# Two feed-forward layers after clustered attention: three chunks of 512 tokens in place of four of 384

## The chip, the cores and the metric

The kernel runs on one core of a Trainium2 chip. The metric is the device time of one execution in microseconds (us). Matrix products run on TensorE (PE; the loads of its stationary operand are listed apart as PEld). VectorE is DVE, ScalarE is ACT, GpSimd is POOL, and SP issues most transfers.

## The reference, cut to what matters

```python
x = attention(q, k, v, centroids)      # 2 x 8 heads x 768 tokens x 64, keys masked by cluster
x = x.reshape(1536, 512)               # tokens x model width
x = (relu(x @ w_in) ** 2) @ w_out      # layer 0: 512 -> 2048 -> 512
h = x @ w_in2
out = (h * sigmoid(1.702 * h)) @ w_out2   # layer 1: 512 -> 2048 -> 512
```

All inputs are float32.

## The kernel before

Each engine executes its instructions in the order in which they are recorded. That order comes from a list of events: `at(key, f)` files a piece of work under a number, the list is sorted by that number, and the pieces are then emitted. Keys are not times; they only decide who stands ahead of whom. Attention has keys up to about 99; for the layers, `moment(u)` turns a position u, counted in units, into a key.

A float32 product is made of three products of rounded parts: every operand is split into a high half (the value rounded to the type float32r) and a low half (value minus high half), and the sum is high x high + low x high + high x low. So each block of a product costs three matmuls.

Tokens are held with the model width on the partitions, in four chunks of 384 (`xhl`, one per half of a batch). The hidden width of 2048 is cut into 16 blocks of 128 (`m`). Each layer has two stretches:

- **Hidden stretch.** For each block m and chunk c one unit: `hidden` issues 12 matmuls (3 products x 4 slices of the model width) into one of eight PSUM banks. `inner` and `outer` apply the activation and store the value in `g_t[m][:, c]`. In layer 0 both run on ACT; in layer 1 ACT makes the sigmoid and DVE multiplies it with the bank.
- **Output stretch.** It is done twice, each time for 768 tokens (g = 0, 1). For each m and half s, `g_high` (ACT) and `g_low` (DVE) split the stored value into the two halves, in a ring of three buffers (`ghl`), and `reduce_out` adds the matmuls of block m into banks that stay open over all 16 blocks. In layer 0 the token chunk is the moving operand (384 columns, line 696); in layer 1 it is the weight tile (512 columns, line 702). Then `leave_high` and `leave_low` write the next layer's x, or `leave` copies a tile of the result, which a transfer takes to memory.

A weight tile (512 x 128 values) comes from memory as 64-bit words. `w_stages` lists its preparation: a transfer of 512 KB by SP into one of two places; `magnitude` on ACT (line 193); `clamp`, `shift`, `join_low`, `join_high` on DVE (lines 196, 200, 204, 208); `high` on ACT (line 212); `low` on POOL (line 215), which subtracts the high half from the value. There are 32 tiles per layer. `weights` files these eight pieces one after another from a position `first` on. Ten places of 4 KB are for tiles; in the output stretch six more tiles lie where chunks 2 and 3 of x lay, and two in places of the w_in tiles.

The first units of layer 0 use batch 0 only and stand among the last pieces of attention: `values` of the last half (24 matmuls into `ps_v`), `ratio`, `whole`, `whole_high`, `whole_low`, whose keys are in the table `LAST`.

Of the kernel before, what the change touches and what calls it, by code (L numbers as in the profile page):

```python
# [8 lines left out]
F32 = mybir.dt.float32  # L9
# [7 lines left out]
P = 128  # L17
# [24 lines left out]
    values=(97.86, 97.96, 98.06, 98.16, 98.26, 98.36), inverse=(95.9, 95.9), spread=(96.2, 96.2), ratio=97.85, ratio_out=98.2,  # L42
    whole=98.9, whole_high=98.95, whole_low=99.2,
# [22 lines left out]
def cluster_attention_then_two_ffns(  # L66
# [30 lines left out]
    NC = B * 2  # L97
# [4 lines left out]
    assert NT == 6 and D == 64 and KD * P == DM and MF == 16 and NC == 4  # L102
# [5 lines left out]
    ROOM = {F32R: 97 * KB, F32: 110 * KB + 512}  # L108
# [51 lines left out]
    g_at = [14 * KB + 512 + 6 * KB * m for m in range(MF)]  # L160
    g_t = [view(a, [NC, HALF]) for a in g_at]
    r_p, tmp, o_p = Places(0, 4608), Places(4608, 4608 + 6 * KB), Places(0, g_at[0])
    words_at = 10 * KB + 512
# [3 lines left out]
    def slot_of(layer, which, m):  # L167

        ring = slots[8:] if layer == 0 else slots[:2]
        rest = slots[:8] if layer == 0 else slots[2:]  # L170
        if which == 0:
            return rest[7] if layer == 0 and m == 2 else ring[m % 2]
        return rest[m] if m < 8 else x_slots[m - 8] if m < 14 else ring[m - 14]

    def weight(layer, which, m):
        return view(slot_of(layer, which, m), [2, DM], F32R)
# [44 lines left out]
    with tc.manual_schedule():  # L221
        with ExitStack() as actx:
# [9 lines left out]
            oht_p = view(12 * KB * 2 + 3 * KB, [S], F32R, 4 * C)  # L232
            oh_p = view(12 * KB * 3 + 3 * KB, [NT, 4, C], F32R)
            ident_r = view(12 * KB * 3 + 4 * KB + 512, [P], F32R)
            oh0_p = view(12 * KB * 2 + 9 * KB, [NT, 4, 2 * C], F32R)
# [350 lines left out]
            def whole(n):  # L586
                p, u = divmod(n, 2)
                b, hp = PAIRS[p]
                x = rb_t[n]
                nc.vector.tensor_tensor(out=x, in0=pv_t.pop(n)[:, :HALF], in1=x, op=ALU.mult)  # L590

            def whole_high(n):
                p, u = divmod(n, 2)
                b, hp = PAIRS[p]
                nc.scalar.copy(out=xhl[2 * b + u][:, 0, hp, :], in_=rb_t[n])

            def whole_low(n):
                p, u = divmod(n, 2)
                b, hp = PAIRS[p]
                x, t = rb_t.pop(n), xhl[2 * b + u]  # L600
                nc.vector.tensor_tensor(out=t[:, 1, hp, :], in0=x, in1=t[:, 0, hp, :].bitcast(F32), op=ALU.subtract)
# [28 lines left out]

            H_LEN, Y_LEN = MF * NC, 2 * MF
            LAYER = H_LEN + 2 * Y_LEN
# [5 lines left out]
            def open_banks():  # L638
                actx.close()
                pool = ctx.enter_context(tc.tile_pool(name="psum2", bufs=1, space=bass.MemoryType.PSUM, reuse_waits="tile"))  # L640
                banks.extend(pool.tile([P, 512], F32, name=f"bank{i}") for i in range(8))

            def bank(i):
                return banks[i % 8]

            def hidden(layer, u, m, c):
                if banks:
                    ps = bank(u)
# [5 lines left out]
                w, x = weight(layer, 0, m), xhl[c]  # L654
# [7 lines left out]
            r_t = {}  # L662

            def inner(layer, m, c):
                r = r_t[layer, m, c] = r_p.tile([P, HALF], F32, tag="r", bufs=3)
                ps = ps_u[layer, m, c][:, :HALF]
                if layer == 0:
                    nc.scalar.activation(out=r, in_=ps, func=AF.Relu)
                else:
                    nc.scalar.activation(out=r, in_=ps, func=AF.Sigmoid, scale=1.702)  # L670

            def outer(layer, m, c):
                r, ps = r_t.pop((layer, m, c)), ps_u.pop((layer, m, c))
                if layer == 0:
                    nc.scalar.activation(out=g_t[m][:, c, :], in_=r, func=AF.Square)
                else:
                    nc.vector.tensor_tensor(out=g_t[m][:, c, :], in0=ps[:, :HALF], in1=r, op=ALU.mult)  # L677


            def half_of(g, m, s):  # L680
                return ghl[((g * MF + m) * 2 + s) % 3]

            def g_high(g, m, s):
                nc.scalar.copy(out=half_of(g, m, s)[:, 0, :], in_=g_t[m][:, 2 * g + s, :])  # L684

            def g_low(g, m, s):
                t = half_of(g, m, s)
                nc.vector.tensor_tensor(out=t[:, 1, :], in0=g_t[m][:, 2 * g + s, :], in1=t[:, 0, :].bitcast(F32), op=ALU.subtract)  # L688

            def reduce_out(layer, g, m, i):  # L690
                w = weight(layer, 1, m)
                if layer == 0:
                    s, d = divmod(i, KD)
                    t = half_of(g, m, s)
                    for e, (a, b) in enumerate(((0, 0), (1, 0), (0, 1))):
                        nc.tensor.matmul(bank(i)[:, :HALF], lhsT=w[:, a, d * P:(d + 1) * P], rhs=t[:, b, :],  # L696
                                         start=(m == 0 and e == 0), stop=(m == MF - 1 and e == 2))
                else:
                    s, i_ = divmod(i, TH)
                    t = half_of(g, m, s)  # L700
                    for e, (b, a) in enumerate(((0, 0), (0, 1), (1, 0))):
                        nc.tensor.matmul(bank(NT * g + i), lhsT=t[:, b, i_ * P:(i_ + 1) * P], rhs=w[:, a, :],  # L702
                                         start=(m == 0 and e == 0), stop=(m == MF - 1 and e == 2))

            def leave_high(g, i):
                s, d = divmod(i, KD)
                nc.scalar.copy(out=xhl[2 * g + s][:, 0, d, :], in_=bank(i)[:, :HALF])

            def leave_low(g, i):
                s, d = divmod(i, KD)  # L710
                x = xhl[2 * g + s]
                nc.vector.tensor_tensor(out=x[:, 1, d, :], in0=bank(i)[:, :HALF], in1=x[:, 0, d, :].bitcast(F32), op=ALU.subtract)

            def leave(g, i):
                o = o_p.tile([P, DM], F32, tag="o", bufs=7)
                rows, ps = out[g * S + i * P:g * S + (i + 1) * P], bank(NT * g + i)
                if g == 1 and i == NT - 1:
# [7 lines left out]
            def weights(layer, which, m, first, pitch=0.3):  # L725
# [108 lines left out]
```

## Time and profile before

| | us |
|---|---|
| median of 3 runs (lowest, highest) | 798.59 (796.96, 798.88) |
| profiled execution: its own time | 797.05 |
| its span, first to last instruction | 795.3 |
| PE busy in the span | 781.6 (98%) |
| DVE, ACT, POOL busy | 460.0, 437.1, 203.4 |

The span is what the profile's rows add up to; what lies around it in the execution's own time is 1.75 us. Busy time of PE says that matmuls are in flight, not that they are at their peak.

### The profile page before, as it was taken

The page shows a single profiled execution, that of the slowest core. Times are in us where ns is not written, and L with a number is a line of the kernel's source. Part 1 is how long each engine was busy: PE and PEld are TensorE (multiplying, and loading weights), DVE is VectorE, ACT ScalarE, POOL GpSimd, SP SyncE. Part 2 cuts the span into 40 slices and gives each one's busy share as a digit, 9 for nine tenths or more (in the row PEclk, how much of TensorE's full clock was granted, in tenths as well). Part 3 has the DMA queues.
Part 4 walks back from the last instruction along what each step waited for, and adds up shares of the span by engine and source line. Part 5 has one row for each costly group of instructions (what it writes and reads, how often), then busy time and mean ns, then how long its engine had stood idle before and what let it go on. Part 6 is the DMA issues. An engine that isn't in the chain of part 4 may idle for free.

```text
span 795.3 us, 12110 instructions
## 1 busy us (share of the span) xinstructions
PE 781.6 (98%) x4523; PEld 685.8 (86%) x4523; DVE 460.0 (58%) x865; ACT 437.1 (55%) x859; POOL 203.4 (26%) x158
## 2 busy tenths in 40 slices
PE   7899999999999999999999999999999999999998
PEld 5766766766776899999999999999999998888886
DVE  6657877877877353545266555755655445663222
ACT  6777887877866476767534344453433333443222
POOL 2564754754601122222011101201211110110000
PEclk9799999999999999999999999999999999999999
DMA  4232332331220133333012201211322101212002
GB/s 140 71 92 58 87 79 56 94 82 46 58 66 28 54 106 107 98 91 130 9 72 80 80 27 55 85 48 56 105 80 78 55 28 54 79 54 80 0 1 80
DMA packets 18202, 54.61 MB, mean 69 GB/s; under 512 B 2720, under 2 KB 2976, under 8 KB 18144
## 3 DMA queue, kind: packets, MB, share of 16 engines
q1 hardware_dynamic: 17856, 53.32, 21.8%
q8 instruction: 35, 0.57, 0.3%
q10 hardware_dynamic: 288, 0.52, 0.2%
q14 instruction: 23, 0.19, 0.1%
HBM read 43.02 MB, written 3.15 MB: 58 GB/s over the span
## 4 chain that ended last, share of the span: by engine, by line
PE 93%; ACT 3%; DVE 2%; issue 1%; POOL 1%; DMA 0%; POOLq 0%; ACTq 0%; DVEq 0%
PE bank L658 31%; PE bank L696 17%; PE bank L702 16%; PE ps_v L562 8%; PE ps_p L544 7%; PE ps_s L519 4%; PE ps_s L522 4%; PE ps_h L658 2%; ACT arena L536 1%; PE ps_aff L380 1%; DVE arena L528 1%; PE ps_r L579 1%; PE ps_back L397 1%; PE ps_oh L463 1%; PE ps_aff L383 0%
## 5 line engine op out<-in xcount | busy, mean ns | idle before, releaser
L658 PE MATMUL bank<-arena 128*128 128x384 f32 x1440 | 249.9, 334 | 0.0
L658 PEld LDWEIGHTS bank<-arena 128*128 128x128 f32 x1440 | 249.6, 188 | 0.0
L215 POOL TENSOR_TENSOR arena<-arena,arena 128x512 fp32r<-128x512 f32 x64 | 82.6, 1291 | 393.8 <-ACT arena L212 349.9
L688 DVE TENSOR_TENSOR arena<-arena,arena 128x384 fp32r<-128x384 f32 x128 | 78.4, 613 | 126.4 <-ACT arena L684 125.3
L684 ACT CAST arena<-arena 128x384 fp32r<-128x384 f32 x128 | 65.8, 514 | 140.5 <-PE bank L702 76.1
L696 PE MATMUL bank<-arena 128*128 128x384 f32 x768 | 133.3, 334 | 0.0
L696 PEld LDWEIGHTS bank<-arena 128*128 128x128 f32 x768 | 133.1, 188 | 0.0
L702 PE MATMUL bank<-arena 128*128 128x512 f32 x576 | 130.8, 389 | 0.0
L702 PEld LDWEIGHTS bank<-arena 128*128 128x128 f32 x576 | 108.1, 188 | 22.4
L528 DVE TENSOR_SCALAR_CACHE_REDUCE arena<-ps_s 128x768 bf16<-128x768 f32 x96 | 91.8, 956 | 43.2 <-PE ps_s L522 37.2
L536 ACT ACTIVATE arena<-ps_s,arena 128x768 f32<-128x768 f32 x96 | 87.0, 906 | 38.2 <-DVE arena L528 37.9
L544 PE MATMUL ps_p<-arena 128*128 128x128 f32 x576 | 72.7, 277 | 0.0
L562 PE MATMUL ps_v<-arena 128*64 128x384 f32 x384 | 72.1, 498 | 0.0
L196 DVE TENSOR_SCALAR arena<-arena 128x512 f32<-128x512 f32 x64 | 34.6, 541 | 61.8 <-ACT arena L193 61.5
L544 PEld LDWEIGHTS ps_p<-arena 128*128 128x128 f32 x576 | 67.8, 144 | 2.4 <-issue 0.6
L677 DVE TENSOR_TENSOR arena<-bank,arena 128x384 f32<-128x384 f32 x64 | 35.6, 556 | 58.9 <-ACT arena L670 58.9
L670 ACT ACTIVATE arena<-bank 128x384 f32<-128x384 f32 x64 | 31.5, 492 | 69.3 <-PE bank L658 69.3
L519 PE MATMUL ps_s<-arena 128*128 128x384 f32 x192 | 55.6, 371 | 4.8 <-ACT arena L536 4.8
L212 ACT CAST arena<-arena 128x512 fp32r<-128x512 f32 x64 | 39.7, 620 | 34.0 <-DVE arena L208 33.9
L522 PE MATMUL ps_s<-arena 80*128 80x384 f32 x192 | 50.9, 346 | 0.6 <-ACT arena L474 0.5
L519 PEld LDWEIGHTS ps_s<-arena 128*128 128x128 f32 x192 | 31.7, 192 | 21.7 <-ACT arena L536 10.1
L552 DVE COPY arena<-ps_p 128x512 f32<-128x512 f32 x72 | 47.0, 677 | 1.0 <-PE ps_p L544 0.9
(95 smaller groups left out, 745.5 us busy)
## 6 DMA issues: line engine op xcount, KB each, us to landing
arena<-in_w_dram SPq DMA_DIRECT2D x64, 512.0 KB, 3.3
arena<-arena SPq DMA_DIRECT2D x32, 192.0 KB, 2.5
arena<-in_k_t_dram SPq DMA_DIRECT2D x8, 384.0 KB, 3.8
arena<-in_v_dram SPq DMA_DIRECT2D x8, 384.0 KB, 3.3
out_dram<-arena SPq DMA_DIRECT2D x11, 256.0 KB, 2.1
arena<-in_q_t_dram SPq DMA_DIRECT2D x7, 384.0 KB, 3.4
arena<-arena SPq DMA_DIRECT2D x28, 48.0 KB, 2.1
arena<-in_q_t_dram ACTq DMA_DIRECT2D x1, 384.0 KB, 3.0
```

What stands on the lines that cost most here:

```text
L215: nc.gpsimd.tensor_tensor(out=halves[:, 1, :], in0=x[0].bitcast(F32), in1=halves[:, 0, :].bitcast(F32), op=ALU.subtract)
L519: nc.tensor.matmul(ps[:, n, :HALF], lhsT=x_s[i][:, t * P:(t + 1) * P], rhs=k1_s[i][:, n * HALF:(n + 1) * HALF], start=True, stop=False)
L522: nc.tensor.matmul(ps[:, n, :HALF], lhsT=q2_s[i][:, t * P:(t + 1) * P], rhs=k2_s[i][:, n * HALF:(n + 1) * HALF], start=False, stop=True)
L528: nc.vector.tensor_scalar(out=unused, in0=s_t[g][:, :, :HALF], scalar1=-scale, scalar2=None, op0=ALU.mult, op1=ALU.min, accum_out=m_t[g])
L536: nc.scalar.activation(out=p_t[g].rearrange("p (n f) -> p n f", n=2), in_=s_t.pop(g)[:, :, :HALF], func=AF.Exp, bias=m_t.pop(g), scale=sca ...
L544: nc.tensor.transpose(ps[:, x * P:(x + 1) * P], p_t[2 * k + j][:, t * P:(t + 1) * P], ident)
L562: nc.tensor.matmul(pv_t[n][j * D:(j + 1) * D, :HALF], lhsT=raw[n // 2, "v"][:, j, t, :], rhs=pt_t[n, j][:, t, :], start=(t == 0), stop=(t ...
L658: nc.tensor.matmul(ps[:, :HALF], lhsT=w[:, a, kk * P:(kk + 1) * P], rhs=x[:, b, kk, :], start=(n == 0), stop=(n == 3 * KD - 1))
L684: nc.scalar.copy(out=half_of(g, m, s)[:, 0, :], in_=g_t[m][:, 2 * g + s, :])
L688: nc.vector.tensor_tensor(out=t[:, 1, :], in0=g_t[m][:, 2 * g + s, :], in1=t[:, 0, :].bitcast(F32), op=ALU.subtract)
L696: nc.tensor.matmul(bank(i)[:, :HALF], lhsT=w[:, a, d * P:(d + 1) * P], rhs=t[:, b, :], start=(m == 0 and e == 0), stop=(m == MF - 1 and e ...
L702: nc.tensor.matmul(bank(NT * g + i), lhsT=t[:, b, i_ * P:(i_ + 1) * P], rhs=w[:, a, :], start=(m == 0 and e == 0), stop=(m == MF - 1 and e ...
```

## The change

The tokens are held as one tensor `xf` (halves x model slices x 1536 tokens) and cut into three chunks of 512. A hidden unit still has 12 matmuls, now 512 columns wide, and there are 48 units per layer, not 64. The output stretch takes chunk 0 alone first (16 units, four banks), then chunks 1 and 2 together (32 units, eight banks), in both layers; its units have 12 matmuls of 512 columns, too. The activation is written to `g_t` in place. Eight w_out tiles (m = 8 to 15) lie where chunks 1 and 2 of x lay, and are prepared while the sums of chunk 0 are made, one every 1.6 units; before, such a tile came every 3.2 units of 12 matmuls of 384 columns. Nine other places hold tiles. Chunk 1 spans both batches, so the first six units stand in another order, and `LAST` has other keys. Every key of the layers' work is new.

```diff
 LAST = dict(
-    values=(97.86, 97.96, 98.06, 98.16, 98.26, 98.36), inverse=(95.9, 95.9), spread=(96.2, 96.2), ratio=97.85, ratio_out=98.2,
-    whole=98.9, whole_high=98.95, whole_low=99.2,
+    values=(97.1, 97.2, 97.3, 97.4, 97.5, 97.6), inverse=(95.9, 95.9), spread=(96.2, 96.2), ratio=97.05, ratio_out=97.4,
+    whole=97.95, whole_high=98.0, whole_low=98.1,
 )
...
-    xhl = [view(12 * KB * c, [2, KD, HALF], F32R) for c in range(NC)]
-    slots = [60 * KB + 4 * KB * i for i in range(7)] + [48 * KB + 4 * KB * i for i in range(3)]
-    x_slots = [24 * KB + 4 * KB * i for i in range(6)]
-    ghl = [view(88 * KB + 3 * KB * i, [2, HALF], F32R) for i in range(3)]
...
+    xf = view(0, [2, KD, B * S], F32R)
+    slots = [view(48 * KB + 4 * KB * i, [2, DM], F32R) for i in range(9)]
+    x_slots = [xf[:, :, kk, c * CH:(c + 1) * CH] for c in (1, 2) for kk in range(KD)]
+    ghl = [view(84 * KB + 4 * KB * i, [2, CH], F32R) for i in range(3)]
...
-                        nc.tensor.matmul(ps[:, :HALF], lhsT=w[:, a, kk * P:(kk + 1) * P], rhs=x[:, b, kk, :],
+                        nc.tensor.matmul(ps, lhsT=w[:, a, kk * P:(kk + 1) * P], rhs=xf[:, b, kk, c * CH:(c + 1) * CH],
...
+            def half_of(m, c):
+                return ghl[(MF + 2 * m + c - 1 if c else m) % 3]
...
+            def sums(layer, c, i):
+                return bank(layer, (0, 4, 8)[c] + i)
+
+            def reduce_out(layer, m, c, i):
+                w, t, ps = weight(layer, 1, m), half_of(m, c), sums(layer, c, i)
+                cols = slice(i * P, (i + 1) * P)
+                for e, (a, b) in enumerate(((0, 0), (1, 0), (0, 1))):
+
+                    lhsT, rhs = (w[:, a, cols], t[:, b, :]) if layer == 0 else (t[:, a, cols], w[:, b, :])
+                    nc.tensor.matmul(ps, lhsT=lhsT, rhs=rhs, start=(m == 0 and e == 0), stop=(m == MF - 1 and e == 2))
...
-            def weights(layer, which, m, first, pitch=0.3):
+            def weights(layer, which, m, first, pitch=0.25):
...
-                at(moment(first - 2.7), load_w)
+                at(moment(first - 1.9), load_w)
...
                     if m >= 8:
-                        jobs.append((y0 + 3.6 + 3.2 * (m - 8), 1, m))
+                        jobs.append((y0 + 0.3 + 1.6 * (m - 8), 1, m))
...
+                    order[:6] = [(0, 0), (1, 0), (0, 1), (1, 1), (0, 2), (1, 2)]
...
+                u = y0
+                for part in PARTS:
                     for m in range(MF):
...
+                        for c in part:
+                            at(moment(u - 1.4), g_high, m, c)
+                            at(moment(u - 1.1), g_low, m, c)
+                            for i in range(4):
+                                at(moment(u + 0.25 * i), reduce_out, layer, m, c, i)
+                            u += 1
```

What this does to the order is seen at two places. On PE, where layer 0 goes from its hidden to its output stretch, before (`bank` is a PSUM bank; x12 counts equal rows in a row):

```order
L658 MATMUL bank6_2697<-arena_99328_58 128x384 x12
L658 MATMUL bank7_2698<-arena_99328_58 128x384 x12
L696 MATMUL bank0_2691<-arena_99328_58 128x384 x3
L696 MATMUL bank1_2692<-arena_99328_58 128x384 x3
L696 MATMUL bank2_2693<-arena_99328_58 128x384 x3
L696 MATMUL bank3_2694<-arena_99328_58 128x384 x3
L696 MATMUL bank4_2695<-arena_99328_58 128x384 x3
```

and at the same place after the change:

```order
L656 MATMUL bank2_2634<-arena_98304_58 128x512 x12
L656 MATMUL bank3_2635<-arena_98304_58 128x512 x12
L695 MATMUL bank4_2636<-arena_98304_58 128x512 x3
L695 MATMUL bank5_2637<-arena_98304_58 128x512 x3
L695 MATMUL bank6_2638<-arena_98304_58 128x512 x3
L695 MATMUL bank7_2639<-arena_98304_58 128x512 x3
L695 MATMUL bank4_2636<-arena_98304_58 128x512 x3
```

Block m = 0 now has four banks and 12 matmuls before block 1 follows in the same banks; before it had eight banks and 24 narrower matmuls.

On ACT, in the first output stretch of layer 0, where w_out tiles are prepared, before (line 193 is `magnitude`, 212 the `high` half of a tile, 684 `g_high`):

```order
L193 ACTIVATE arena_59<-arena_59 128x512
L684 CAST arena_58<-arena_59 128x384
L212 CAST arena_58<-arena_59 128x512
L684 CAST arena_58<-arena_59 128x384 x2
L193 ACTIVATE arena_59<-arena_59 128x512
```

and after (191, 210 and 679 are the same three), around the tile m = 13, whose `high` is the first of the two rows of line 210:

```order
L191 ACTIVATE arena_59<-arena_59 128x512
L679 CAST arena_58<-arena_59 128x512
L210 CAST arena_58<-arena_59 128x512
L679 CAST arena_58<-arena_59 128x512
L191 ACTIVATE arena_59<-arena_59 128x512
L679 CAST arena_58<-arena_59 128x512 x2
L210 CAST arena_58<-arena_59 128x512
```

The `g_high` behind that `high` is the one of unit 11 of the 16. DVE does for the same tile, after the change (194 `clamp`, 198 `shift`, 202 and 206 the joins, 683 `g_low`):

```order
L194 TENSOR_SCALAR arena_59<-arena_59 128x512
L198 TENSOR_SCALAR arena_59<-arena_59 128x512
L683 TENSOR_TENSOR arena_58<-arena_59,arena_58 128x512
L202 SCALAR_TENSOR_TENSOR arena_59<-arena_59 128x512
L206 SCALAR_TENSOR_TENSOR arena_59<-arena_59 128x512
L683 TENSOR_TENSOR arena_58<-arena_59,arena_58 128x512
L194 TENSOR_SCALAR arena_59<-arena_59 128x512
```

Per tile there are now one or two `g_low` between one `clamp` and the next, the second of the two here being that of unit 11; before there were about three.

## Rows read from the trace of the kernel before

**Rows 1.** The page: busy time, share of the span and instructions of each engine.

```profile
PE 781.6 (98%) x4523; PEld 685.8 (86%) x4523; DVE 460.0 (58%) x865; ACT 437.1 (55%) x859; POOL 203.4 (26%) x158
```

**Rows 2.** End of the chain that ended last: start us, us, engine, tile, line, count.

```profile
256.68 4.38 PE ps_h L658 x24
261.39 4.02 PE ps_v L562 x24
265.41 12.70 PE ps_h L658 x72
278.12 116.48 PE bank L658 x672
394.60 133.12 PE bank L696 x768
527.72 133.12 PE bank L658 x768
660.83 130.62 PE bank L702 x576
```

**Rows 3.** Groups by line and shape: count, busy us, mean ns, idle us before.

```profile
L658 PE MATMUL bank<-arena 128*128 128x384 f32 x1440 | 249.9, 334 | 0.0
L702 PE MATMUL bank<-arena 128*128 128x512 f32 x576 | 130.8, 389 | 0.0
```

**Rows 4.** Busy time by stretch: us, PE, PEld, DVE, ACT, POOL (instructions), clock, DMA.

```profile
256.60:394.30 137.70, 137.70 (x797) 135.10 (x796) 60.60 (x98) 89.24 (x176) 29.72 (x23) 1.00 0.26 85
394.30:527.30 133.00, 133.00 (x769) 133.00 (x768) 78.81 (x140) 57.23 (x111) 20.62 (x16) 1.00 0.21 68
...
791.40:795.30 3.90, 0.04 (x1) 0.00 (x0) 0.42 (x1) 0.37 (x1) 0.00 (x0) 1.00 0.64 232
```

**Rows 5.** Instructions in order of time, 401 to 407 us, one w_out tile.

```profile
401.12 0.67 ACT L193 ACTIVATE arena<-arena 128x512 f32<-128x512 f32 x1
...
401.82 0.43 DVE L196 TENSOR_SCALAR arena<-arena 128x512 f32<-128x512 f32 x1
402.28 0.43 DVE L200 TENSOR_SCALAR arena<-arena 128x512 int32<-128x512 int32 x1
402.74 0.69 DVE L204 SCALAR_TENSOR_TENSOR arena<-arena 128x512 int32<-128x512 int32 x1
...
403.35 0.55 DVE L688 TENSOR_TENSOR arena<-arena,arena 128x384 fp32r<-128x384 f32 x1
403.82 0.69 DVE L208 SCALAR_TENSOR_TENSOR arena<-arena 128x512 int32<-128x512 int32 x1
404.54 0.62 ACT L212 CAST arena<-arena 128x512 fp32r<-128x512 f32 x1 [1.25 <-DVE arena L208]
...
405.07 0.51 ACT L684 CAST arena<-arena 128x384 fp32r<-128x384 f32 x1
405.24 1.29 POOL L215 TENSOR_TENSOR arena<-arena,arena 128x512 fp32r<-128x512 f32 x1 [22.19 <-ACT arena L212]
405.61 1.33 DVE L688 TENSOR_TENSOR arena<-arena,arena 128x384 fp32r<-128x384 f32 x1 [1.10 <-ACT arena L684]
```

**Rows 6.** DVE in order of time, 268 to 269 us: joins back to back.

```profile
268.17 0.69 DVE L204 SCALAR_TENSOR_TENSOR arena<-arena 128x512 int32<-128x512 int32 x1
268.90 0.69 DVE L208 SCALAR_TENSOR_TENSOR arena<-arena 128x512 int32<-128x512 int32 x1
```

**Rows 7.** Single lines: duration ns min/median/max, first and last start.

```profile
L196 DVE TENSOR_SCALAR arena<-arena x64: 427/428/1067, 235.0 to 712.9; 128x512 f32<-128x512 f32 x64
...
L688 DVE TENSOR_TENSOR arena<-arena,arena x128: 548/559/1341, 391.4 to 785.7; 128x384 fp32r<-128x384 f32 x128
...
L677 DVE TENSOR_TENSOR arena<-bank,arena x64: 545/558/558, 531.7 to 661.4; 128x384 f32<-128x384 f32 x64
```

**Rows 8.** POOL and DVE in order of time, near 280 us.

```profile
279.79 1.30 POOL L215 TENSOR_TENSOR arena<-arena,arena 128x512 fp32r<-128x512 f32 x1 [6.04 <-ACT arena L212]
...
280.30 1.07 DVE L196 TENSOR_SCALAR arena<-arena 128x512 f32<-128x512 f32 x1 [1.90 <-ACT arena L193]
```

**Rows 9.** Transfers: line, queue, count, KB each, median us to landing.

```profile
arena<-in_w_dram SPq DMA_DIRECT2D x64, 512.0 KB, 3.3
```

More of the change, by code (lines that the diff above doesn't have):

```diff
@@ L640, in open_banks, with bank @@
                 pool = ctx.enter_context(tc.tile_pool(name="psum2", bufs=1, space=bass.MemoryType.PSUM, reuse_waits="tile"))
-                banks.extend(pool.tile([P, 512], F32, name=f"bank{i}") for i in range(8))
-            def bank(i):
-                return banks[i % 8]
+                banks.extend(pool.tile([P, CH], F32, name=f"bank{i}") for i in range(8))
+            def bank(layer, i):
+                return banks[(i + (4, 0)[layer]) % 8]
             def hidden(layer, u, m, c):
                 if banks:
-                    ps = bank(u)
+                    ps = bank(layer, u)
                 else:
@@ L653, in hidden @@
                 ps_u[layer, m, c] = ps
-                w, x = weight(layer, 0, m), xhl[c]
+                w = weight(layer, 0, m)
                 n = 0
@@ L667, in inner @@
                 if layer == 0:
-                    nc.scalar.activation(out=r, in_=ps, func=AF.Relu)
+                    nc.scalar.activation(out=g, in_=ps, func=AF.Relu)
                 else:
-                    nc.scalar.activation(out=r, in_=ps, func=AF.Sigmoid, scale=1.702)
+                    nc.scalar.activation(out=g, in_=ps, func=AF.Sigmoid, scale=1.702)
             def outer(layer, m, c):
-                r, ps = r_t.pop((layer, m, c)), ps_u.pop((layer, m, c))
+                g, ps = g_t[m][:, c, :], ps_u.pop((layer, m, c))
@@ L674, in outer @@
                 if layer == 0:
-                    nc.scalar.activation(out=g_t[m][:, c, :], in_=r, func=AF.Square)
+                    nc.scalar.activation(out=g, in_=g, func=AF.Square)
                 else:
[L677 to L714, printed above, removed]
+                    nc.vector.tensor_tensor(out=g, in0=ps, in1=g, op=ALU.mult)
@@ new lines, in half_of, with g_high, g_low @@
+            def half_of(m, c):
+                return ghl[(MF + 2 * m + c - 1 if c else m) % 3]
+            def g_high(m, c):
+                nc.scalar.copy(out=half_of(m, c)[:, 0, :], in_=g_t[m][:, c, :])
+            def g_low(m, c):
+                t = half_of(m, c)
+                nc.vector.tensor_tensor(out=t[:, 1, :], in0=g_t[m][:, c, :], in1=t[:, 0, :].bitcast(F32), op=ALU.subtract)
+            def sums(layer, c, i):
[6 more added lines that the diff above has]
+                    nc.tensor.matmul(ps, lhsT=lhsT, rhs=rhs, start=(m == 0 and e == 0), stop=(m == MF - 1 and e == 2))
@@ L715, in leave, with leave_high, leave_low @@
+            def leave_high(c, d):
+                nc.scalar.copy(out=xf[:, 0, d, c * CH:(c + 1) * CH], in_=sums(0, c, d))
+            def leave_low(c, d):
+                x = xf[:, :, d, c * CH:(c + 1) * CH]
+                nc.vector.tensor_tensor(out=x[:, 1], in0=sums(0, c, d), in1=x[:, 0].bitcast(F32), op=ALU.subtract)
+            def leave(c, i):
                 o = o_p.tile([P, DM], F32, tag="o", bufs=7)
-                rows, ps = out[g * S + i * P:g * S + (i + 1) * P], bank(NT * g + i)
@@ L717, in leave @@
-                if g == 1 and i == NT - 1:
+                t = c * (CH // P) + i
+                rows, ps = out[t * P:(t + 1) * P], sums(1, c, i)
+                if t == B * NT - 1:
                     for copy, dma, cols in ((nc.scalar.copy, nc.scalar, slice(0, DM // 2)), (nc.vector.tensor_copy, nc.sync, slice(DM // 2, DM))):
@@ L723, in leave @@
                 nc.sync.dma_start(out=rows, in_=o)
-            def weights(layer, which, m, first, pitch=0.3):
-                h = first - LAYER * (first >= LAYER)
-                hidden_now = h < H_LEN
+            def weights(layer, which, m, first, pitch=0.25):
                 n = turns[0] = turns[0] + 1
-                place = words_at if n % 2 else g_at[15] if hidden_now else 0
-                load_w, parts = w_stages(layer, which, m, place)
-                at(moment(first - 2.7), load_w)
+                load_w, parts = w_stages(layer, which, m, words_at[n % 2])
+                at(moment(first - 1.9), load_w)
                 for x, f in enumerate(parts):
```

104 lines of the change are left out of this document (45 added, 59 removed).

## The prediction

> **What bounds the kernel now.** The page comes first: PE is busy for 98% of the span, the other engines for 58% or less [rows 1]. That says only that matmuls are in flight, so the chain that ended last is read next, for what the end waits on [rows 2]. From 256.68 us on it is PE alone. Each segment starts where the one before ended (278.12 + 116.48 = 394.60; 394.60 + 133.12 = 527.72; then 660.84), up to 791.45, with 4.0 us of attention's `values` and a short `ratio` among the first. Neither layer has an idle microsecond, and the groups of lines 658 and 702 show 0.0 idle, too [rows 3]. So the 530 us of the layers are the number of matmuls times the spacing at which PE takes them. The chain gives it for two widths: 133.12/768 = 173.3 ns for 384 columns (line 658 in layer 1, line 696 in layer 0), and 130.62/576 = 226.8 ns for 512 (line 702). Third, the table by stretch: the granted clock is 1.00, the 2.4 GHz level, and in the first output stretch DVE and ACT are busy for 78.8 and 57.2 of 133 us [rows 4]. On average they have room; whether they keep the order in which PE wants things is the question below.
>
> **The matmuls.** Before, layers 0 and 1 issue 1,536 hidden and 768 output matmuls of 384 columns and 576 of 512. After, there are 1,152 hidden and 1,152 output ones, all of 512. The columns are the same; 576 matmuls are gone. 2,304 x 173.3 = 399.4 us and 1,728 x 226.8 = 391.9 us, so PE needs 7.5 us less. The price of the new width isn't extrapolated: line 702 has the very shape, a loaded 128x128 and a moving 128x512. From 384 to 512 columns the spacing grows by 53.5 ns, 2.39 columns per ns; the other 13 ns come with each matmul whatever its width, and 576 x 13 = 7.5.
>
> The Trainium skill speaks against this term: "TensorE: Matmul & The Clock Gate", section "Back-to-back issue gap", gives N/2.4 + 2.5 ns for matmuls at the full clock, so only 2.5 ns of each would not be columns; by it the 576 matmuls are worth 1.4 us. The rows above do not agree with it here, at either width.
>
> **What costs nothing while PE covers it.** In the hidden stretch ACT is busy for 89 of 138 us with 64 units [rows 4]; 48 wider ones have a fixed part less often, so its load falls. A unit is 12 x 0.2268 = 2.72 us, three of them (8.16 us) for one block as against four of 2.08 (8.32) before, so w_in tiles are due at nearly the old pace, and a transfer takes 3.3 us [rows 9] of the 5.2 us (1.9 units) between its issue and `magnitude`. In the last pieces of attention one unit of 2.72 us stands ahead of `values` where two of 2.08 us stood; `whole_high` of the last half now stands ahead of unit 0's square on ACT and holds it until `values` is done, about 4 us. Banks of those units come free late, but bank 0 is wanted again only four units, 11 us, later; without that cover the loss would be the 4 us. Chunk 2 of the sums takes the banks of chunk 0 one unit after they end, 2.7 us for four casts on ACT and four subtractions on DVE of 0.55 to 0.7 us each; it also holds. The tail behind the last matmul keeps its split copy and its two transfers, 3.9 us as now [rows 4].
>
> **The stretch of chunk 0.** Here a cost appears. A w_out tile is due every 1.6 units, 4.35 us; before it was every 3.2 units of 2.08, 6.66 us. The preparation is a loop: `high` waits for DVE, the next `magnitude` stands behind `high` on ACT, and DVE waits for that `magnitude`. And DVE is held by POOL: the `g_low` that started at 405.61 inside POOL's subtraction (405.24 to 406.53) ended 0.41 us behind it and took 1.33 us, not 0.56 [rows 5]; a `clamp` started inside one (279.79 to 281.09) ended 0.28 behind it [rows 8]. The longest `g_low` and `clamp` are 1,341 and 1,067 ns, while line 677, one of whose inputs lies in PSUM, never goes over 558 [rows 7].
>
> Count from the start H of a `high`. POOL starts at H + 0.70 and ends at H + 1.99 [rows 5]. The next `magnitude` can start 0.53 later than H, the `clamp` 0.70 after it (401.12 to 401.82), or 0.53 more if a `g_high` is between; either way inside POOL's time, so it ends at H + 2.27 and `shift` starts at 2.30. Then 0.46 to the first join, 0.73 to the second (268.17 to 268.90 [rows 6]), 0.72 to the next `high` [rows 5]: 4.21. Into this fall 1.6 `g_low` per tile. One that cuts into the chain costs 0.36 (between the joins: 0.61 + 0.47 in place of 0.73 [rows 5]) to 0.5; one that stands ahead of the `clamp` is itself held by POOL and makes the period about 4.84. Along the order after the change I count one in nearly every period: 4.72 to 4.84, **4.77** as a mean. It is more than 4.35, so the tiles fall back by 0.42 us each.
>
> Who waits? The `g_high` of unit 11 stands right behind the `high` of tile 13, the sixth. The first `high` comes 4.5 us after the stretch begins (0.7 until `magnitude`, 3.1 for the chain, 0.7 for a `g_low` in it). The sixth is at 4.5 + 5 x 4.77 = 28.35. The `g_high` starts 0.53 later and takes 0.62 (as line 212, which is as wide), so `g_low` starts at 29.54, inside POOL's time (29.05 to 30.34), and ends some 0.54 behind it, at 30.9. PE wants it for the third matmul of unit 11: 11 x 2.72 + 0.45 = 30.4. PE waits 0.5 to 0.6 us. Unit 12, whose `g_low` stands behind the joins of tile 14, waits another 0.15. Unit 3 had the same place behind the first `high` with 5 x 0.42 = 2.1 us more to spare; the next would be unit 19, when the tiles are done. So 0.7 us a layer, 1.4 in both.
>
> Bounds: with a period up to 4.65 unit 11 waits for nothing; with all 1.6 `g_low` at 0.5 the period is 5.0, unit 11 waits 5 x 0.35 = 1.75, and two more tiles add up to 2 x 0.65: 3 us a layer, 6 in all. I take 1.4, since the steps come from rows of the same loop.
>
> **Sum.** 797.05 - 7.5 + 1.4 = 790.95 against the profiled execution. That one is 1.5 us below the median of the runs shown and 0.1 above the lowest; the middle of all four times is 797.8, and from there it is **791.7 us**.
>
> **Rivals.**
> - *No wait in the chunk-0 stretch* (period under 4.65): 797.8 - 7.5 = 790.3. For it: the average room of DVE; against it: the held instructions of rows 5 and 8.
> - *The loop is slower*, 4.85 to 5.1: 2.5 to 6 us given back, 792.8 to 796.3. For it: two `g_low` in some periods.
> - *The spacing goes with the columns alone*: 512 of them would take 173.3 x 512/384 = 231.1 ns, nothing is gained, and 797.8 + 1.4 = 799.2, the same. The 226.8 of line 702 speaks against it. (By the page of the Trainium skill named above it would come out 1.4 us lower.)
> - *Slower than before:* the same loop at 5.4 us. To lose 2.4 us net, 9.9 us of waits are needed, 5 a layer: 5 x (p - 4.65) + 2 x (p - 4.35) = 5 gives p = 5.3 as the point from which it decides; at 5.4 it is 5.9 a layer, 802. It needs POOL to hold DVE twice in a period, or a `high` to wait for a second `g_high`. Nothing in the rows does.
>
> **How the numbers follow.** 0.3% of 798 is 2.4 us, about what a measurement of this kernel can tell from no change. Chances: the forecast 0.50, no wait 0.22, slower loop 0.17 (0.13 of it still faster by over 0.3%), columns only or a loop of 5.1 to 5.3 together 0.06, slower 0.05. Faster 0.85, same 0.10, slower 0.05. The range goes from no wait, less the 1 us by which the times of one kernel differ, to a loop of about 5.05: 789.2 to 795.6.
>
> **What would show it.** In the profile after: 2,304 matmuls of 512 columns at 226 to 227 ns in the chain; no idle of PE in the hidden stretches and in those of chunks 1 and 2; about 0.7 us of PE idle near the eleventh unit of chunk 0 in each layer, put down to `g_low` on DVE; more `g_low` and `clamp` of over 1 us than now; tiles at 4.7 to 4.8 us. The prediction is wrong if the hidden matmuls are further apart than 227 ns, if PE waits at the hand-over from attention, or if the waits in the two stretches are over 3 us each.

## The result, and the profile after

| | us |
|---|---|
| before, median of 4 runs (lowest, highest) | 798.52 (796.96, 798.88) |
| after, median of 4 runs (lowest, highest) | 790.76 (790.19, 790.93) |
| ratio, 95% interval | 0.9906 [0.9891, 0.9922] |
| profiled execution after: its own time, its span | 790.69, 788.9 |

The kernel is 0.9% faster. Between the two profiled executions the span falls by 6.4 us, from 795.3 to 788.9. The page of the kernel after gives the busy time, share and instructions of each engine, and its costliest groups (busy us, mean ns of one, idle us before them):

```profile
PE 775.4 (98%) x3947; PEld 610.5 (77%) x3947; DVE 457.6 (58%) x813; ACT 418.2 (53%) x775; POOL 203.3 (26%) x158
...
L695 PE MATMUL bank<-arena 128*128 128x512 f32 x1152 | 262.3, 389 | 0.6 <-DVE arena L683 0.6
L656 PE MATMUL bank<-arena 128*128 128x512 f32 x1104 | 250.6, 389 | 0.0
```

PE still has its 98%, with 576 matmuls fewer than in [rows 1]; the share alone tells nothing of the gain. New is an idle time of 0.6 us ahead of the output matmuls (line 695, both layers now), put down to DVE's `g_low` (line 683). Where it lies is seen when PE is listed in order of time (start us, us, engine, line, tiles, count, [idle before]); this answers to [rows 2]. First comes the row of the kernel before with which its layers begin in this listing, then the kernel after:

```profile
256.61 4.45 PE L658 MATMUL ps_h<-arena 128*128 128x384 f32 x24
```

```profile
256.45 3.04 PE L656 MATMUL ps_h<-arena 128*128 128x512 f32 x12
...
263.77 8.46 PE L656 MATMUL ps_h<-arena 128*128 128x512 f32 x36
272.07 119.84 PE L656 MATMUL bank<-arena 128*128 128x512 f32 x528
391.75 30.54 PE L695 MATMUL bank<-arena 128*128 128x512 f32 x134
422.56 100.62 PE L695 MATMUL bank<-arena 128*128 128x512 f32 x442 [0.28 <-DVE arena L683]
523.02 130.72 PE L656 MATMUL bank<-arena 128*128 128x512 f32 x576
653.58 30.31 PE L695 MATMUL bank<-arena 128*128 128x512 f32 x133
684.22 100.84 PE L695 MATMUL bank<-arena 128*128 128x512 f32 x443 [0.34 <-DVE arena L683]
```

Read the starts, not the durations, since neighbours overlap by 0.16 us. The hidden stretch of layer 1 lasts 653.58 - 523.02 = 130.56 us, 226.7 ns for each of 576 matmuls. The output stretch of layer 0 has as many and lasts 523.02 - 391.75 = 131.27, so 0.71 us are lost in it. That of layer 1 ends at 785.06 and lasts 131.48; as the last row of a listing is whole, its measure is 130.72, and 0.76 are lost. The list breaks off after 134 matmuls: 11 units of 12 and two, so the third of unit 11 waited. Without a wait it would have started at 391.75 + 134 x 0.2267 = 422.12; it started at 422.56, so 0.44 us went there. The row's idle of 0.28 is less by the 0.16 of the usual overlap. The rest, nearly 0.3 us, went in the matmuls right behind it and at unit 12. There a load of the stationary operand waited for `g_low`, too, as PEld in order of time shows (the second row starts with unit 12's third load):

```profile
422.56 2.60 PEld L695 LDWEIGHTS bank<-arena 128*128 128x128 f32 x12 [0.70 <-DVE arena L683]
425.42 14.61 PEld L695 LDWEIGHTS bank<-arena 128*128 128x128 f32 x65 [0.26 <-DVE arena L683]
```

In layer 1 the list breaks off after 133, since there the low half of the activation is wanted by the second matmul of a unit.

What unit 11 waited for, from the instructions of all engines around 421 us:

```profile
419.24 0.69 DVE L206 SCALAR_TENSOR_TENSOR arena<-arena 128x512 int32<-128x512 int32 x1
419.97 0.62 ACT L210 CAST arena<-arena 128x512 fp32r<-128x512 f32 x1 [3.00 <-DVE arena L206]
...
420.49 0.62 ACT L679 CAST arena<-arena 128x512 fp32r<-128x512 f32 x1
420.66 1.30 POOL L213 TENSOR_TENSOR arena<-arena,arena 128x512 fp32r<-128x512 f32 x1 [3.40 <-ACT arena L210]
...
421.14 1.37 DVE L683 TENSOR_TENSOR arena<-arena,arena 128x512 fp32r<-128x512 f32 x1 [1.21 <-ACT arena L679]
```

The `high` of tile 13 (line 210) starts at 419.97, the `g_high` of unit 11 right behind it at 420.49, and its `g_low` at 421.14, inside POOL's subtraction (420.66 to 421.96). It takes 1.37 us and ends 0.55 behind POOL's end. Each of the eight subtractions of POOL in this stretch holds one instruction of DVE: four times a `g_low` (about 1.37 us), four times a `clamp` (1.06). The period of the loop, from one `high` to the next, is 4.83 us where a `g_low` is held and 4.70 where a `clamp` is. Without the hold this `g_low` of 0.69 us would have ended at 421.83, before PE wanted it at 422.12: unit 11 waits because the loop is late and because its own `g_low` is held. The lines of the two alone answer to [rows 7] (min/median/max ns):

```profile
L683 DVE TENSOR_TENSOR arena<-arena,arena x96: 674/692/1420, 388.8 to 777.6; 128x512 fp32r<-128x512 f32 x96
```

```profile
L194 DVE TENSOR_SCALAR arena<-arena x64: 412/427/1069, 235.1 to 687.7; 128x512 f32<-128x512 f32 x64
```

The tail is as before: last matmul at 785.06, end of span at 788.9.

### The profile page after: what moved, and what is told of

The parts are those of the page before. It is cut to its first block, busy times and chain, and to the rows that moved or that the text cites. A ratio compares the mean times of both kernels' runs of the same rounds, so it can differ in the third digit from the quotient of the medians.

```text
span 788.9 us, 10653 instructions
## 1 busy us (share of the span) xinstructions
PE 775.4 (98%) x3947; PEld 610.5 (77%) x3947; DVE 457.6 (58%) x813; ACT 418.2 (53%) x775; POOL 203.3 (26%) x158
## 4 chain that ended last, share of the span: by engine, by line
PE 88%; DVE 6%; ACT 3%; issue 1%; POOL 1%; DMA 0%; ACTq 0%; DVEq 0%; POOLq 0%
PE bank L656 32%; PE bank L695 28%; PE ps_v L560 8%; PE ps_p L542 7%; PE ps_s L517 5%; PE ps_s L520 4%; PE ps_h L656 1%; DVE arena L683 1%; ACT arena L534 1%; PE ps_aff L378 1%; DVE arena L526 1%; PE ps_r L577 1%; DVE arena L206 1%; DVE arena L194 1%; DVE arena L202 1%
## 5 line engine op out<-in xcount | busy, mean ns | idle before, releaser
L695 PE MATMUL bank<-arena 128*128 128x512 f32 x1152 | 262.3, 389 | 0.6 <-DVE arena L683 0.6
L695 PEld LDWEIGHTS bank<-arena 128*128 128x128 f32 x1152 | 215.9, 188 | 46.7 <-DVE arena L683 2.0
L656 PE MATMUL bank<-arena 128*128 128x512 f32 x1104 | 250.6, 389 | 0.0
L656 PEld LDWEIGHTS bank<-arena 128*128 128x128 f32 x1104 | 207.2, 188 | 43.0
L683 DVE TENSOR_TENSOR arena<-arena,arena 128x512 fp32r<-128x512 f32 x96 | 74.8, 781 | 106.4 <-ACT arena L679 105.1
L679 ACT CAST arena<-arena 128x512 fp32r<-128x512 f32 x96 | 59.1, 619 | 105.0 <-PE bank L695 105.0
L194 DVE TENSOR_SCALAR arena<-arena 128x512 f32<-128x512 f32 x64 | 38.4, 599 | 73.7 <-ACT arena L191 73.7
L210 ACT CAST arena<-arena 128x512 fp32r<-128x512 f32 x64 | 39.6, 618 | 64.9 <-DVE arena L206 64.9
L665 ACT ACTIVATE arena<-bank 128x512 f32<-128x512 f32 x48 | 28.7, 598 | 79.0 <-PE bank L656 79.0
L672 DVE TENSOR_TENSOR arena<-bank,arena 128x512 f32<-128x512 f32 x48 | 33.1, 690 | 58.0 <-ACT arena L665 58.0
L202 DVE SCALAR_TENSOR_TENSOR arena<-arena 128x512 int32<-128x512 int32 x64 | 45.3, 708 | 2.0
L206 DVE SCALAR_TENSOR_TENSOR arena<-arena 128x512 int32<-128x512 int32 x64 | 44.2, 691 | 1.9
```

The costliest lines, as they stand in the source:

```text
L202: nc.vector.scalar_tensor_tensor(out=x[0], in0=words[:, :, 0], scalar=29, in1=x[0], op0=ALU.logical_shift_right, op1=ALU.bitwise_or)
L656: nc.tensor.matmul(ps, lhsT=w[:, a, kk * P:(kk + 1) * P], rhs=xf[:, b, kk, c * CH:(c + 1) * CH], start=(n == 0), stop=(n == 3 * KD - 1))
L679: nc.scalar.copy(out=half_of(m, c)[:, 0, :], in_=g_t[m][:, c, :])
L683: nc.vector.tensor_tensor(out=t[:, 1, :], in0=g_t[m][:, c, :], in1=t[:, 0, :].bitcast(F32), op=ALU.subtract)
L695: nc.tensor.matmul(ps, lhsT=lhsT, rhs=rhs, start=(m == 0 and e == 0), stop=(m == MF - 1 and e == 2))
```

## The experiments

The theory, A: the spacing has about 13 ns that do not depend on the width, so 576 matmuls fewer save about 7.5 us; and 0.7 us per layer go back because the loop that prepares a w_out tile takes 4.76 us, with POOL's subtraction holding DVE, where 4.35 are due. The rivals are stated in the expectations; B is that the wait comes from one awkward place in the order, without any backlog of the loop. Spans and stretches are read as above, from starts to starts: an output stretch without waits lasts 130.56 us in layer 0 and, with the last row whole, 130.72 in layer 1. Changes are to the kernel after.

**Tiles further apart.** One number, so that they are due every 1.7 units, 4.62 us:

```diff
-                        jobs.append((y0 + 0.3 + 1.6 * (m - 8), 1, m))
+                        jobs.append((y0 + 0.3 + 1.7 * (m - 8), 1, m))
```

> The changed kernel with its eight w_out tiles one every 1.7 units (4.62 us), not 1.6 (4.35 us). Theory A (a loop of 4.76 us per tile that POOL lengthens, so tiles fall back by 0.4 us each until PE waits): the tiles fall back by only 0.14 us each, 0.7 us over five; both waits of PE in the two chunk-0 stretches vanish and the span falls by 0.9 to 1.5 us, to 787.4 to 788.0. Theory B (the wait is one awkward place in the order, units 11 and 12, without any backlog): a wait of some tenths stays or shows at other units; span 788.3 to 789.2.

Its own time was 791.40. PE in order of time, and two rows of ACT:

```profile
258.62 3.04 PE L656 MATMUL ps_h<-arena 128*128 128x512 f32 x12
...
393.92 130.72 PE L695 MATMUL bank<-arena 128*128 128x512 f32 x576
524.48 130.72 PE L656 MATMUL bank<-arena 128*128 128x512 f32 x576
655.04 130.72 PE L695 MATMUL bank<-arena 128*128 128x512 f32 x576
```

```profile
419.54 0.61 ACT L679 CAST arena<-arena 128x512 fp32r<-128x512 f32 x1
...
422.76 0.62 ACT L210 CAST arena<-arena 128x512 fp32r<-128x512 f32 x1 [2.61 <-DVE arena L206]
```

Both output stretches are one row of 576 matmuls, with no wait, and the layers are 1.5 us shorter (785.76 - 258.62 = 527.14, after 785.06 - 256.45 = 528.61). After a first step of 5.31 us the loop kept its period of 4.70 to 4.83. The `high` of tile 13 even starts later in the stretch than in the changed kernel (422.76 - 393.92 = 28.84 us, after 28.22), and nobody waits, because the `g_high` of unit 11 now stands ahead of it (419.54). The edit moved the pieces in the order as well as the pace. So A's number came, but this run alone does not tell a smaller backlog from a better place in the order. The span missed what I expected: attention ended 2.2 us later in this execution, which is taken up in the last section.

**Tiles closer together.** The same number at 1.3 units, 3.54 us. In this kernel some words of a tile are another tile's, since a transfer is filed ahead of the last reading of the words that lie in its place.

> The changed kernel with the tiles one every 1.3 units (3.54 us). Theory A: the loop can't go faster than 4.7 us, so the tiles fall back by 1.2 us each and PE waits at most units from 3 to 12, 13 to 15 us in each layer; span 814 to 819, slower than the kernel before. Theory B: DVE is asked for 2.35 us per tile and 0.9 for its share of subtractions, 3.25 us, less than 3.54, so it keeps up: span 788 to 791.

The time was 818.32 and the output stretches 145.46 and 145.11 us, inside what I had expected, but not for that reason: DVE also waited for the transfers (the view of waits, engine and line waited for, us in total, times, longest, 391 to 440 us):

```profile
DVE arena L202 <- DMA arena<-in_w_dram: 9.2, 6, 1.8
```

And part of the loss is no wait at all. Behind two waits of PE of 2.91 and 3.00 us the granted clock fell, part of the time to the 1.2 GHz level (PE in order of time, then a stretch as in [rows 4]):

```profile
410.28 6.88 PE L695 MATMUL bank<-arena 128*128 128x512 f32 x22 [2.91 <-DVE arena L683]
...
428.44 108.76 PE L695 MATMUL bank<-arena 128*128 128x512 f32 x466 [3.00 <-DVE arena L683]
```

```profile
427.00:436.00 9.00, 7.56 (x21) 5.96 (x22) 6.94 (x12) 3.92 (x7) 2.57 (x2) 0.62 0.17 60
```

At 226.7 ns each, and with the 0.16 of overlap, the two rows would have lasted 5.1 and 105.8 us; so some 4.7 of the 14.9 us lost in layer 0 lie inside them. A second wait and a lower clock had come in with the order, so the number proves nothing. The same at 1.45 units, with the same remark on the words of some tiles:

> The changed kernel with its w_out tiles one every 1.45 units (3.95 us). Theory A: the tiles fall back by 0.8 us each instead of 0.4; PE waits 3 to 6 us in each layer (output stretches of 133.5 to 136.5 us, as against 131.3 to 131.5 in the changed kernel), which puts the run at 5 to 9 us over the changed kernel, about the time of the kernel before. Theory B: DVE is asked for 3.35 us in 3.95, keeps up, 131 to 132.

It took 798.38, with stretches of 133.33 and 136.79 us. Layer 1 loses 3.3 us more than layer 0, and its view of waits (655 to 692 us) has one wait for a transfer; behind it the granted clock is 0.72 from 684 to 690 us:

```profile
DVE arena L206 <- DMA arena<-in_w_dram: 2.8, 1, 2.8
```

Both were therefore made again with the transfers filed later, behind the last reading:

```diff
-                at(moment(first - 1.9), load_w)
+                at(moment(first - (1.55 if which == 1 and m >= 8 else 1.9)), load_w)
```

(1.55 with tiles every 1.3 units; 1.85 with tiles every 1.45.)

> The changed kernel with its w_out tiles one every 1.3 units, as in the run before at that distance, but each tile's transfer filed 1.55 units ahead of it and so behind the last reading of the words that lay in its place. Counted are the two output stretches (130.56 us without a wait; 145.5 and 145.1 at this distance with the transfer filed 1.9 units ahead). Theory A, a loop of 4.7 to 4.8 us held by POOL: the tiles come every 4.75, not every 3.54 us; PE waits about 5 us in each layer, 135 to 136; the other 10 us of the run before came from DVE's joins waiting for a transfer. Theory C (the 15 us were all POOL's and the loop's): 143 to 146 again.

> The changed kernel with its w_out tiles one every 1.45 units and their transfers filed 1.85 units ahead. Theory A: the loop stays at 4.7 to 4.8 us where 3.95 is asked; PE waits about 3 us in each layer, both output stretches 133 to 134 us (the 136.8 us of layer 1 in the run before at this distance held a wait for a transfer). Theory C: 133.3 and 136.8 again.

At 1.3 units: 801.05, stretches of 135.44 and 135.67. At 1.45: 796.52, 133.37 and 133.54. Layer 0 of the first, PE in order of time:

```profile
393.71 19.38 PE L695 MATMUL bank<-arena 128*128 128x512 f32 x84
413.56 0.73 PE L695 MATMUL bank<-arena 128*128 128x512 f32 x2 [0.47 <-ACT arena L679]
414.74 5.71 PE L695 MATMUL bank<-arena 128*128 128x512 f32 x24 [0.44 <-DVE arena L683]
421.35 3.03 PE L695 MATMUL bank<-arena 128*128 128x512 f32 x12 [0.90 <-DVE arena L683]
424.86 3.06 PE L695 MATMUL bank<-arena 128*128 128x512 f32 x12 [0.47 <-DVE arena L683]
428.82 100.49 PE L695 MATMUL bank<-arena 128*128 128x512 f32 x442 [0.91 <-DVE arena L683]
529.15 130.72 PE L656 MATMUL bank<-arena 128*128 128x512 f32 x576
```

The granted clock stays at 1.00 in both. The loop did not get slower (4.22 to 4.71, and 4.69 to 4.83); what is due moved, and with it the places in the order. The loss per layer goes 0, 0.7, 2.8, 4.9 us for tiles due every 4.62, 4.35, 3.94 and 3.54 us. Of the 14.9 us that the first of the 1.3-unit kernels lost in layer 0, about 10 went when its transfers were filed later: the waits for transfers and the time at the lower clock together. The same loop that costs the change 0.7 us a layer takes the whole gain away when tiles are asked for every 3.54 us: 9.8 us in both layers, where fewer matmuls save 7.7. (The times, one run each, were 801.05 and 799.59 for the kernel before.)

**POOL's subtraction left out,** for the eight tiles in question; their low halves are then not computed.

```diff
-        return load, [magnitude, clamp, shift, join_low, join_high, high, low]
+        return load, [magnitude, clamp, shift, join_low, join_high, high] + [low] * (which == 0 or m < 8)
```

> The changed kernel without POOL's subtraction for w_out tiles 8 to 15 of both layers (their low halves are left out: the matmuls read what lay there). DVE and ACT do what they did. Theory A: without POOL nothing holds DVE, the loop is 4.35 us or less, no g_low or clamp of over 1 us is left in the two stretches, PE doesn't wait; span 787.4 to 788.0. Theory B, or a loop bound by its own steps: the period stays over 4.6 us and a wait of 0.3 us or more stays in each layer; span 788.4 to 789.2.

It took 791.38 (unit 0 at 258.62, the late start again). The stretches have no wait:

```profile
393.91 130.72 PE L695 MATMUL bank<-arena 128*128 128x512 f32 x576
...
655.03 130.72 PE L695 MATMUL bank<-arena 128*128 128x512 f32 x576
```

The loop's period in layer 0 falls from 4.76 to 4.15 us (4.06 to 4.25), less than the 4.35 that are due, and every `g_low` and `clamp` of the stretch is back at 0.69 and 0.43 us. No step of ACT or DVE was taken out and their order is the same, so the 0.6 us are what POOL's subtraction adds to the loop, through DVE. This run speaks against B, too: with the pieces of unit 11 at the same place in the order, its `g_low` now ends 27.0 us into the stretch, 3.4 before PE wants it. Holding that one instruction, 0.7 us, could not have made PE wait; the backlog is needed as well.

**The subtraction twice,** for the same eight tiles:

```diff
-        return load, [magnitude, clamp, shift, join_low, join_high, high, low]
+        return load, [magnitude, clamp, shift, join_low, join_high, high, low] + [low] * (which == 1 and m >= 8)
```

> The changed kernel with POOL's subtraction issued twice for w_out tiles 8 to 15 of both layers (the second writes the same values again). DVE and ACT do what they did; POOL, busy for 10 of 44 us there, has room for it. Counted from the first output matmul of a layer to its last stretch's end, 130.6 us without any wait and 131.3 to 131.5 in the changed kernel. Theory A (POOL holds DVE and so lengthens the loop, now by 1.3 us more, to about 5.3 to 6): PE waits 6 to 8 us in each layer, 137 to 139; the sum is 12 to 14 us longer than the changed kernel, and the run slower than the kernel before. Theory B (POOL beside the path): 131 to 132, no change.

It took 806.63, with the kernel before at 798.45 beside it (unit 0 at 258.11, late again). The period is 5.81 us (5.67 to 5.93), and the stretches last 138.58 and 138.47: 8.0 and 7.75 us lost, at a granted clock of 1.00. POOL, and PE in layer 0, in order of time:

```profile
421.88 2.72 POOL L213 TENSOR_TENSOR arena<-arena,arena 128x512 fp32r<-128x512 f32 x2 [2.93 <-ACT arena L210]
```

```profile
393.40 14.21 PE L695 MATMUL bank<-arena 128*128 128x512 f32 x62
407.82 5.75 PE L695 MATMUL bank<-arena 128*128 128x512 f32 x24 [0.20 <-DVE arena L683]
414.68 6.19 PE L695 MATMUL bank<-arena 128*128 128x512 f32 x24 [1.11 <-DVE arena L683]
421.81 3.02 PE L695 MATMUL bank<-arena 128*128 128x512 f32 x12 [0.94 <-DVE arena L683]
...
531.98 130.72 PE L656 MATMUL bank<-arena 128*128 128x512 f32 x576
```

None, one or two subtractions give 4.15, 4.76 and 5.81 us a tile. POOL is busy for under 3 us of each period and never the bound; it costs through the engine that it holds.

**Half the width.** The hidden matmuls of layer 0 as two halves of 256 columns, one half after the other: twice the matmuls, the same columns.

```diff
-                for a, b in ((0, 0), (1, 0), (0, 1)):
-                    for kk in range(KD):
-                        nc.tensor.matmul(ps, lhsT=w[:, a, kk * P:(kk + 1) * P], rhs=xf[:, b, kk, c * CH:(c + 1) * CH],
...
+                for lo, hi in ((0, CH),) if layer else ((0, CH // 2), (CH // 2, CH)):
+                    n = 0
+                    for a, b in ((0, 0), (1, 0), (0, 1)):
+                        for kk in range(KD):
+                            nc.tensor.matmul(ps[:, lo:hi], lhsT=w[:, a, kk * P:(kk + 1) * P], rhs=xf[:, b, kk, c * CH + lo:c * CH + hi],
...
```

> The changed kernel with every hidden matmul of layer 0 in two halves of 256 columns, first all twelve of one half and then all twelve of the other: 576 matmuls of 512 become 1,152 of 256, the columns stay. Theory A1 (each matmul costs about 13 ns beside its columns, at any width): 256 columns take 120 ns, the stretch grows by 1,152 x 120 - 576 x 226.7 = 7.7 us; span 796 to 798. Theory A2 (below some width the load of the stationary operand sets the spacing, and the 173.3 ns of 384 columns were already such a load): 173.3 ns each at 256 columns, too; the stretch grows by 69 us; span 857 to 859.

It took 797.99, with a span of 796.2. PE in order of time:

```profile
272.30 126.88 PE L658 MATMUL bank<-arena 128*128 128x256 f32 x1056
399.02 30.56 PE L697 MATMUL bank<-arena 128*128 128x512 f32 x134
```

(399.02 - 272.30)/1056 = 120.0 ns. The three widths of 256, 384 and 512 columns now give 120.0, 173.3 and 226.7 ns: 53.3 ns for every 128 columns, and 120.0 - 2 x 53.3 = 13.3 ns with each matmul at any of them. In [rows 4] the loads (PEld) were busy for all 133.00 us at 384 columns, which looked as if they were the limit there; but they do not set the spacing even at 120 ns.

**The split of the activation earlier.** `g_high` and `g_low` are filed half a unit sooner, which changes neither the pieces of the loop nor when a tile is due:

```diff
-                            at(moment(u - 1.4), g_high, m, c)
-                            at(moment(u - 1.1), g_low, m, c)
+                            at(moment(u - 1.9), g_high, m, c)
+                            at(moment(u - 1.6), g_low, m, c)
```

> The changed kernel with the tiles as they are, one every 1.6 units, but g_high and g_low half a unit earlier in the order (1.9 and 1.6 units ahead of their matmuls, not 1.4 and 1.1). Theory A with its place (the g_high of unit 11 waits because it stands right behind the high of the sixth tile, which the loop has made late): it now stands ahead of that high, the loop stays at 4.7 to 4.8 us but PE doesn't wait; both output stretches 130.6 us. If the backlog reached PE by any way (the tiles themselves, or DVE's load), waits of 0.4 us or more stay in each layer.

It took 788.94, with a span of 787.1:

```profile
256.15 3.04 PE L656 MATMUL ps_h<-arena 128*128 128x512 f32 x12
...
391.45 130.72 PE L695 MATMUL bank<-arena 128*128 128x512 f32 x576
...
652.57 130.72 PE L695 MATMUL bank<-arena 128*128 128x512 f32 x576
```

The loop still has 4.70 to 4.83 us, its sixth `high` starts 27.96 us into the stretch, and nobody waits. So the slow loop alone costs nothing here; it costs where the pieces of a unit stand behind it.

**The changed kernel again, and the better pitch, timed.** The changed kernel as it is, and tiles every 1.7 units, six runs each beside ten of the kernel before:

> The changed kernel once more, beside the next one on the same chip: 0.9906 of the kernel before within the interval measured first (0.989 to 0.992).

> The changed kernel with the tiles one every 1.7 units, timed: by theory A its layers are 1.4 to 1.5 us shorter (0.18%), so a ratio about 0.002 below that of the changed kernel beside it; theory B: the same ratio.

| | median us (lowest, highest) | ratio to before, 95% interval |
|---|---|---|
| before | 798.45 (796.36, 799.47) | |
| changed kernel | 790.7 (790.1, 792.93) | 0.9912 [0.9895, 0.9928] |
| tiles every 1.7 units | 790.43 (788.8, 791.7) | 0.9903 [0.9886, 0.992] |

The first result repeats. The waits are gone in the profile of the second (span 787.0, both output stretches rows of 576 matmuls), but its median lies only 0.3 us below, inside the intervals: the start of the layers differs from run to run by more than the 1.5 us that the waits cost. Three of its six times (788.8 to 789.46) lie below all of the changed kernel's, three above all but one (791.4 to 791.7). The gain of the 1.7 is shown in the traces and not settled by the times.

## Why the prediction was right

**The matmuls.** The spacing was foretold as 226.8 ns and measured 226.7, and the saving came. It is 2,304 x 173.33 - 1,728 x 226.67 ns = 7.7 us; the 7.5 of the prediction was 0.2 too small, because its 226.8 came from a row of the chain, which is counted from end to end and not between starts. The reason given for it, 13 ns with each matmul whatever its width, is shown by a third width that no trace of before had (13.3 at 256 columns). The prediction weighed N/2.4 + 2.5 ns from the Trainium skill's "TensorE: Matmul & The Clock Gate", section "Back-to-back issue gap". It left out that the section gives this for an isolated matmul, and for streams of loads and matmuls, which these are, about 131 ns at 512 columns. The trace agrees with neither, and the measurement decides: 226.7 ns at 512 columns, and 13.3 that are not columns, five times the 2.5. The rival "columns alone" fell by the same three spacings, which do not grow in proportion to the columns.

**The sum, checked.** From one profiled execution to the other the span fell by 6.4 us. The terms: 7.7 us of matmuls gone, 0.71 + 0.76 = 1.5 of waits back, 0.2 because unit 0 began earlier (256.61 before, 256.45 here): 6.4 us less. The forecast of 6.1 from profiled to profiled thus held by its terms. The medians differ by 7.8, 1.4 more. Of the 14 times of the kernel before in the two tables, nine lie at 798.35 or above and five at 796.96 or below; of the ten of the changed kernel, one lies at 792.93 and nine at 790.93 or below. The profiled pair (797.05 and 790.69) goes with the two lower groups. Why the groups are so unequal isn't shown, and whether the change has a part in it was not tried. That the median of 790.76 came within 1 us of the forecast of 791.7 is therefore in part luck; it even lies nearer to the rival "no wait" (790.3). It is the trace, and not the time, that shows the waits.

**The stretch of chunk 0.** The loop was put at 4.77 us and has 4.76 in the changed kernel; the sixth `high` at 28.35 us of the stretch, and it started at 28.22 (419.97 - 391.75). PE waited where it was said, at the third matmul of unit 11 (in layer 1 the second), and a little at unit 12, for 0.7 us a layer. One held instruction per period and periods of 4.72 to 4.84 were counted; it is one in each, with 4.70 and 4.83. The cause given, POOL's subtraction holding `g_low` and `clamp`, is shown by taking it out (4.15 us, no wait) and doubling it (5.81). That the place in the order is needed too is shown by moving the split ahead. The Trainium skill's "SBUF — State Buffer", section "Who interferes with whom", says that a VectorE instruction with two SBUF inputs contends with a GpSimd instruction that reads SBUF, and that the port pair they share is an exclusive lock. The held `g_low` has two such inputs and agrees (1.37 us inside the subtraction, 0.69 without it). That sentence does not speak of the `clamp`, which has one input and was held as well (1.06 us, where 0.43 is usual). The runs show the holding, not the port.

**What was to cost nothing.** No idle of PE at the hand-over from attention, in the hidden stretches, or at the change of banks to chunks 1 and 2: the rows of PE run through. What any of these would have cost without its cover was not tried. The tail measured 3.8 us against 3.9.

**The rivals.** "No wait" was to need a period under 4.65: with 4.15 it came true. It isn't the only way: at 1.7 units, and with the split filed earlier, PE does not wait either, at the same period of 4.7 to 4.83 and in another order. "Slower than before" was to decide from a period of 5.3 on; at 5.81 the kernel was slower by 8 us, and the formula given, 5 x (5.81 - 4.65) + 2 x (5.81 - 4.35) = 8.7 us a layer, is near the 8.0 and 7.75 measured. One more subtraction of POOL per tile was enough for it.

## What to carry to other kernels

Price a merge of matmuls by the spacing at two widths in the kernel's own trace: what doesn't grow with the columns is what fewer, wider ones save. When preparation runs as a loop over several engines, compare the loop's period, and not the busy shares, with the pace at which its results are due, and look at which consumer stands right behind a step of the loop in an engine's order; filing that consumer a little earlier can remove the wait without making the loop faster. An engine that is busy for 26% of the span can still lengthen that period, through the engine that it holds.

## What was not expected of the hardware

Times of one kernel lie up to 3 us apart (before: 796.36 to 799.47; tiles every 1.7 units: 788.8 to 791.7), and the profiles place this ahead of the layers. Of two executions of the kernel with tiles every 1.7 units, one began unit 0 at 258.62 and the other at 256.00. The first, by stretch (us, busy time of PE, PEld, DVE, ACT, POOL, granted clock, DMA):

```profile
36.00:42.00 6.00, 5.20 (x33) 3.00 (x33) 3.15 (x7) 5.88 (x12) 5.32 (x4) 1.00 0.30 67
42.00:48.00 6.00, 4.30 (x19) 2.21 (x20) 0.00 (x0) 2.22 (x5) 3.45 (x3) 0.72 0.20 42
```

and the second:

```profile
36.00:42.00 6.00, 4.16 (x29) 2.00 (x27) 2.14 (x4) 4.95 (x9) 5.92 (x4) 1.00 0.39 89
42.00:48.00 6.00, 5.50 (x40) 3.77 (x41) 2.05 (x5) 3.10 (x7) 2.27 (x2) 1.00 0.15 29
```

In both PE had waited 2.3 us for POOL. In the first the granted clock of the next stretch is 0.72, part of it at the 1.2 GHz level, and pairs of matmuls of 384 columns still take 0.85 us behind the wait:

```profile
43.70 0.86 PE L381 MATMUL ps_aff<-arena 128*32 128x384 f32 x2 [2.34 <-POOL arena L371]
...
45.64 0.85 PE L378 MATMUL ps_aff<-arena 128*32 128x384 f32 x2
```

In the second it is 1.00, and from 43.92 us on such pairs take 0.5. The stretch from POOL's line 362 to its line 571 lasts 15.4 us in the first (37.10 to 52.49) and 13.9 in the second (35.91 to 49.80); the rest of the lateness, 1.2 us, is there already at the first of these lines. The profiles of the other kernels agree. Of all thirteen, five have 0.72 from 42 to 48 us, and begin unit 0 at 258.11 to 258.62; the eight with 1.00 begin it at 256.00 to 256.79, four of them although the clock was 0.72 to 0.77 in the stretch of 36 to 42 us. Why the same program is granted the full clock there in one execution and not in the other stays open; it was not tried.
